# First unit's last pair with gates of its own, second unit's decays moved behind the first unit's masks, later weight merges on GpSimd

## The chip, the cores and the metric

The kernel runs on one core of one Trainium2 chip. The metric is the device time of one execution in microseconds (us); the time before is the median of three runs, 569.17 us (569.11 to 569.18). The profile is one execution under the hardware profiler, whose span is 567.4 us at a granted TensorE clock of 0.996. Engines: PE is TensorE, DVE is VectorE, ACT is ScalarE, POOL is GpSimd, SP is SyncE, which here only issues transfers.

## The reference, cut to what matters

The first half is a gated linear recurrence per batch entry and head, the second half a two-layer network with an ELU between the layers.

```python
f = 1.0 / (1.0 + np.exp(-f_logit))
for t in range(S):
    state = f[:, :, t, :, None] * state + np.einsum('bhd,bhe->bhde', k[:, :, t], v[:, :, t])
    y[:, :, t] = np.einsum('bhd,bhde->bhe', q[:, :, t], state)
h = x @ w_in
g = np.where(h > 0.0, h, alpha * (np.exp(np.minimum(h, 0.0)) - 1.0))
return (g @ w_out).astype(np.float32)
```

Sizes: 4 batch entries, 8 heads, 768 tokens, head size 48; x has 3072 rows of 384, the inner width is 2048. q, k, v and f_logit arrive as fp32, the weights as float64, and the kernel turns the weights into fp32 on the chip.

## The kernel before, in words

**Units.** The tokens are cut into 12 units of 256 (three per batch entry). For each unit q, k and f lie as 128 partitions x 4 head pairs x 256 tokens. 48 of every 64 partitions are real data, 16 are a gap. For f, the fourth pair (index `NKT` = 3) is not loaded into its own place before: its 96 rows go into the gaps beside the other three pairs (`load`, L437), so that the gates (exp and add) and the running products treat three pairs of 128 full partitions, and `move` (L629 to L634), an SBUF-to-SBUF transfer in two parts, then brings the result to the fourth pair's place.

**One unit's recurrence.** `gates` forms 1 + exp(-f_logit) on ACT (L608, L610). `grow` (L622) is a running product over the 256 tokens on DVE, `fall` (L627) its reciprocal on DVE. `scale` (L617) multiplies k by the product and q by its reciprocal on GpSimd. `transposed` (L665, L669) turns the scaled k on PE and copies it out on ACT, `advance` (L724) forms the state updates on PE, `step` (L682, L684, L687) sums them on DVE (the first one on ACT), `scores` (L701) is q times k on PE, `mask` (L709) applies the causal triangle on DVE. `outputs` and `carried` (L739, L759) form the unit's rows of x on PE, and ACT copies them out (L766, L768). For the very first unit `first_outputs` (L804 to L816) does the last two. `watch` (L646) only keeps a flag on the running products being in range.

**Weights.** Each of the 16 weight items (a 384 x 256 block of w_in, or a 256 x 384 block of w_out) is float64 when it lands in `area`, a ring of `AHEAD` = 7 places. `split` (L559, L563: two tensor_scalar operations on DVE) and `lower` (L569, ACT) prepare it, and `merge` (L577) adds the two 32-bit parts into the fp32 weight and then issues the fetch of the item seven further on. In order of need the items are: 0 wi0, 1 wi1, 2 wi2, 3 wo0, 4 wi3, 5 wo1, 6 wi4, 7 wo2, 8 wi5, 9 wo3, and so on. Before, all merges are on DVE: the integer add compiles to a custom DVE operation over 16-bit halves.

**Order.** Before the main loop the operations are written out by hand (L1037 to L1117); each engine runs its part in that order, and the SP queue issues transfers in that order. The main loop counts steps T. At even T = 2P it runs `up(P)` (x times a w_in block, L923 for the first two units), at odd T `down(P - 2)` (L955). A dictionary `plan` holds what else is done at which step: `attention(1, (), A1)` plans unit 1's advance, steps, scores with mask, outputs and carried at the steps named in A1, and `merge(n)` is planned two steps ahead of the item's first use, split and lower two steps before that. `warm` (L1032) are multiplications without a use that only keep TensorE busy. From unit 2 on, `up7` and `down` work with seven products instead of eight; that part isn't touched.

**DMA bookkeeping.** All transfers, of SP and of ACT, share eight completion semaphores in turn, so a transfer's issue waits until the transfer that had the same semaphore before it has landed. On the SP queue everything behind such an issue waits too.

Of the kernel before, what the change touches and what calls it, by code (L numbers as in the profile page):

```python
# [9 lines left out]
I32 = mybir.dt.int32  # L10
# [346 lines left out]
def fast(ctx: ExitStack, tc: tile.TileContext, q, k, v, f_logit, w_in, w_out, out, flag, outer):  # L357
# [36 lines left out]
    LAG = 2  # L394
    AHEAD = 7
    WA = 1
    W0 = 3
    HOLD = 2
    A1 = (2, 4, 4, 5, 7, 9)
    D2 = (14, 16, 18, 20)  # L400
    A2 = (22, 24, 24, 26, 27, 28)
    D3 = (-7, -5, -3, -1)
# [25 lines left out]
    def load(u, names="fkqv"):  # L428
        b, s0 = u // UPB, (u % UPB) * U
        for n in names.replace("v", ""):  # L430
            to = qkf[u % NB][n][MAIN]
            frm = src[n][b, :, :, s0 : s0 + U].rearrange("(p r) d s -> (r d) p s", r=2)
            if n == "f":
                to, frm = to[:, 0:NKT, 0], frm[:, 0:NKT]
            nc.sync.dma_start(out=to, in_=frm)
            for r in range(2 if n == "f" else 0):
# [14 lines left out]
    def blank(i, *engines, zeros=None):  # L451
        for j, e in enumerate(engines):
            w = HP // len(engines)
            for n in "kq":
                e.memset(qkf[i][n][:, j * w : (j + 1) * w], 0.0)
        (zeros or engines[-1]).memset(qkf[i]["f"][:, NKT], 1.0)

    start = ctx.enter_context(ExitStack())
    start.enter_context(tc.manual_schedule())
# [105 lines left out]
    def lower(n):  # L565

        if wide and n < NFT:
            raw = raws[n]
            nc.scalar.activation(raw.bitcast(U16)[:, 2::4], raw.bitcast(U32)[:, 0::2], AF.Copy, scale=2.0**-29)  # L569

    def merge(n):
        if wide and n < NFT:
            hi = raws.pop(n).bitcast(I32)[:, 1::2]
            j, out_ = parts[n]
            to = wo[:, 2 * j : 2 * j + 2] if out_ else wi[j][:]
            bits, hi = (x.rearrange("p (k f) -> p k f", k=to.shape[1]) for x in (held.pop(n)[:], hi))
            nc.vector.tensor_tensor(out=to.bitcast(I32), in0=bits, in1=hi, op=ALU.add)  # L577
        fetch(n + AHEAD)


# [22 lines left out]
    def gates(u, pieces=(NKT,), bias=1):  # L603

        p = 0
        for n in pieces:
            a = qkf[u % NB]["f"][:, p : p + n, 0]
            nc.scalar.activation(a, a, AF.Exp, scale=-1.0)  # L608
            if bias:
                nc.scalar.activation(a, a, AF.Copy, bias=1.0)  # L610
            p += n

    def scale(u, *todo):

        t = qkf[u % NB]
        for n, p, e in todo:
            e.tensor_tensor(out=t[n][:, p], in0=t[n][:, p], in1=t["f"][:, p, "kq".index(n)], op=ALU.mult)  # L617
# [27 lines left out]
    def watch(u):  # L645
        nc.vector.scalar_tensor_tensor(  # L646
            out=fine[:], in0=qkf[u % NB]["f"][:, 0:NKT, 0, U - 1 :], scalar=LIMIT, in1=fine[:],
            op0=ALU.is_le, op1=ALU.mult,
        )

# [39 lines left out]
    def scores(u, banks=("a0", "a1"), pairs=range(HP), pc=None):  # L690

        t = qkf[u % NB]
        if pc is None:
            ats[u] = sb.tile([128, 2, NW, HP, C], FP32, tag="at", name=f"at{u}", bufs=1)
            pc = [ps.tile([128, NW, HP, C], FP32, tag=banks[r], name=f"psS{u}_{r}") for r in range(2)]
        for p in pairs:
            for w in range(NW):
                for b in range(2):
                    cols = slice(w * W + b * C, w * W + b * C + C)
                    for r in range(2):  # L700
                        nc.tensor.matmul(  # L701
                            pc[r][FULL[b], w, p], lhsT=t["k"][FULL[r], p, cols], rhs=t["q"][FULL[r], p, cols],
                            start=True, stop=True,
                        )
        return pc
# [8 lines left out]
    def advance(u, pairs=range(HP)):  # L714

        if u not in pus:
            pus[u] = [ps.tile([128, NW, HP, D], FP32, tag=n, name=f"psU{u}_{n}") for n in ("a0", "a1")]
        pu = pus[u]
        for p in pairs:
            for w in range(NW):  # L720
                for r in range(2):
                    h = 2 * p + r
                    for b in range(2):
                        nc.tensor.matmul(  # L724
                            pu[b][FULL[r], w, p], lhsT=kns[u, p // 2][FULL[b], p % 2, w, FULL[r]],
                            rhs=vs[u % NB][FULL[b], w, PAD + h * D : PAD + (h + 1) * D],
                            start=(w == 0 and p == 0), stop=(w == NW - 1 and p == HP - 1), skip_group_check=True,
                        )
# [91 lines left out]
    def at_step(step, *todo):  # L820
        plan.setdefault(step, []).extend(todo)
# [206 lines left out]
    def warm(n, bank="m0"):  # L1028

        pw = ps.tile([128, 4, 128], FP32, tag=bank, name="psW")  # L1030
        for _ in range(n):
            nc.tensor.matmul(  # L1032
                pw[:], lhsT=ident[:], rhs=ident[:].unsqueeze(1).broadcast_to([128, 4, 128]), start=True, stop=True
            )


    gates(0, (1, 2))  # L1037
    fetch(0)
    load(1, "kqv")
    for n in range(1, HOLD):  # L1040
        fetch(n)
    warm(W0, "m3")
    for p in range(NKT):
        grow(0, p)
        scale(0, ("k", p, nc.gpsimd))
        if p < 2:
            transposed(0, 0, "m0", (p,))
    move(0, 0, nc.scalar)
    transposed(0, 1, "m1", (0,))
    fall(0, 0)  # L1050
    scale(0, ("q", 0, nc.gpsimd))
    warm(WA, "m3")
# [5 lines left out]
        vs[0][:, :, PAD : PAD + NKT * 2 * D].rearrange("t w (p r d) -> t w p r d", r=2, d=D)[:, :, :, 0],  # L1058
    )
    fall(0, 1)  # L1060
    scale(0, ("k", NKT, nc.gpsimd), ("q", 1, nc.gpsimd))
    fall(0, 2)
    move(0, 1, nc.scalar)
    warm(4)
    transposed(0, 1, "m1", (1,))
    advance(0, (2,))
    scores(0, None, (1,), pc)
    scale(0, ("q", 2, nc.gpsimd))
    advance(0, (3,))
    scores(0, None, (2,), pc)  # L1070
    nc.gpsimd.tensor_copy(
        padded_v[:, :, :, PAD : 2 * PAD].rearrange("t w (r j) k -> t w r j k", r=2),
        vs[0][:, :, PAD + NKT * 2 * D : PAD + DM].rearrange("t w (r k j) -> t w r j k", r=2, j=NKT),
    )
    a = qkf[1]["f"][:, 0:NKT, 0]
    nc.vector.tensor_scalar_add(a, a, 1.0)
    for p in range(NKT):
        grow(1, p)
    move(1, 0, nc.sync)
    scale(0, ("q", NKT, nc.gpsimd))  # L1080
    warm(2)
    scores(0, None, (NKT,), pc)
    warm(1)
    fall(1, 0)
    for c in range(NC - 1):
        step(0, c)
    mask(0, pc)
    step(0, NC - 1)
    split(0)
    for c in range(NC - 1):  # L1090
        nc.gpsimd.tensor_copy(
            padded_s[:, c, :, PAD : 2 * PAD],
# [4 lines left out]
        nc.gpsimd.memset(area[:, HOLD:].bitcast(I32)[:, :, 0:1], 0)  # L1097
# [12 lines left out]
    transposed(1, 1, "a1")  # L1110
    lower(1)
    watch(0)
    scale(1, ("q", 1, nc.gpsimd))
    fall(1, 2)
    scale(1, ("q", 2, nc.gpsimd))
    move(1, 1, nc.scalar)
    watch(1)  # L1117
    at_step(1, lambda: scale(1, ("q", NKT, nc.gpsimd)))
    attention(1, (), A1)
    for n in range(1, NFT):  # L1120
        t = max(needs[n][0] - 2, 0)
        at_step(t, lambda n=n: merge(n))
        if n > 1:
            later.setdefault(max(t - 2, 0), []).append(n)
    at_step(4, lambda: load(2))
# [89 lines left out]
```

## Time and profile before

| | us |
|---|---|
| time, median of three | 569.17 |
| span in the profile | 567.4 |
| PE busy | 550.2 (97%) |
| DVE busy | 395.2 (70%) |
| POOL busy | 266.3 (47%) |
| ACT busy | 229.3 (40%) |

The averages hide two stages. Up to some 45 us the recurrence of units 0 and 1 and the conversion of the first weights run, and PE waits now and then; from there on PE is without a gap up to the last microseconds. The page shows this in its 40 slices of 14.2 us: the first three digits of PE are 6, 8 and 7, all but the last of the others are 9. So the times of day in the first 60 us, in the timeline of each engine, are what has to be read: start, length, engine, line, tile, and in brackets how long the engine stood still before and what released it. A line of the DMA queue (SPq, ACTq) is the issue of a transfer, not the transfer.

### The profile page before, as it was taken

Reading aid. Unit: us, or ns where it says so; the run is one execution under the profiler, and the core shown is the slowest. Engines: PE = TensorE matmul, PEld = TensorE weight load, DVE = VectorE, ACT = ScalarE, POOL = GpSimd, SP = SyncE. Lnnn points to the kernel's source line nnn. Section 1 sums busy time; section 2 is a strip of 40 time slices with the busy share of each in tenths; the row PEclk is TensorE's granted clock in tenths of the full one; section 3 lists DMA queues with packets and bytes.
Section 4 is the critical chain, followed back from the end, with each engine's and each line's share of the span. In section 5 each row is a group of like instructions: output and inputs, shape, how many; then the busy total and the mean of one; then the engine's idle time right before and its main releaser. Section 6 shows DMA issues by size and latency. Waiting matters only on the chain.

```text
span 567.4 us, 15202 instructions
## 1 busy us (share of the span) xinstructions
PE 550.2 (97%) x6226; PEld 501.8 (88%) x6226; DVE 395.2 (70%) x765; ACT 229.3 (40%) x417; POOL 266.3 (47%) x530
## 2 busy tenths in 40 slices
PE   6879999999999999999999999999999999999996
PEld 3457777778999999999999999999999999999995
DVE  8798485835976795885785885786786876745543
ACT  3297737334343443434333343343333343333331
POOL 6510027642374474465366357257257348325332
PEclk9998999999999999999999999999999999999999
DMA  8989780060025125215216216216206203201001
GB/s 207 259 215 297 174 223 14 2 161 29 2 50 140 58 60 143 73 45 152 79 36 155 85 37 154 84 38 154 84 20 172 84 9 72 85 2 36 29 2 35
DMA packets 37902, 53.27 MB, mean 94 GB/s; under 512 B 3680, under 2 KB 27648, under 8 KB 37824
## 3 DMA queue, kind: packets, MB, share of 16 engines
q1 hardware_dynamic: 37024, 51.62, 34.6%
q8 instruction: 51, 0.84, 0.6%
q10 hardware_dynamic: 800, 0.59, 0.5%
q14 instruction: 27, 0.22, 0.1%
HBM read 44.04 MB, written 4.72 MB: 86 GB/s over the span
## 4 chain that ended last, share of the span: by engine, by line
PE 92%; DVE 3%; DMA 2%; issue 1%; ACT 1%; POOL 1%; SPq 0%; DVEq 0%; ACTq 0%; POOLq 0%
PE psH L878 35%; PE psM L977 33%; PE psM L955 8%; PE psH L923 6%; PE psS L701 2%; PE psY L739 2%; PE psY L759 2%; PE psU_a L724 2%; PE psT L665 2%; DMA f<-f 1%; DVE f L627 1%; DMA f<-in_f_logit_dram 1%; ACT area L569 1%; DVE bits L559 0%; PE psY L804 0%
## 5 line engine op out<-in xcount | busy, mean ns | idle before, releaser
L878 PE MATMUL psH<-xt,wi 128*128 128x128 f32 (+1 forms) x960 | 177.1, 293 | 0.0
L942 POOL TENSOR_TENSOR sums<-gg 128x128 f32<-128x128 f32 x160 | 69.5, 455 | 210.8 <-DVE gg L932 202.5
L878 PEld LDWEIGHTS psH<-xt,wi 128*128 128x128 f32 x960 | 135.9, 192 | 0.8
L910 ACT ACTIVATE gg<-hh 128x512 f32<-128x512 f32 x80 | 50.5, 631 | 205.9 <-DVE hh L900 140.5
L878 PE MATMUL psH<-xt,area 128*128 128x128 f32 x640 | 110.5, 275 | 0.0
L878 PEld LDWEIGHTS psH<-xt,area 128*128 128x128 f32 x640 | 96.9, 192 | 4.1
L887 DVE TENSOR_TENSOR hh<-psH,u 128x256 f32<-128x256 f32 x80 | 33.8, 423 | 88.7 <-ACT u L885 88.7
L977 PE MATMUL psM<-area,sums 128*128 128x192 f32 x480 | 91.2, 326 | 0.0
L977 PEld LDWEIGHTS psM<-area,sums 128*128 128x128 f32 x480 | 80.1, 190 | 0.2 <-POOL sums L942 0.2
L977 PE MATMUL psM<-wo,gg 128*128 128x192 f32 x320 | 68.1, 335 | 0.0
L617 POOL TENSOR_TENSOR k<-k,f 128x256 f32<-128x256 f32 x48 | 39.4, 822 | 57.1 <-DMA area<-in_moe_w_in_dram 35.0
L627 DVE RECIPROCAL f<-f 128x256 f32<-128x256 f32 x36 | 62.8, 1747 | 1.3
L911 ACT ACTIVATE gg<-gg 128x512 f32<-128x512 f32 x96 | 60.6, 631 | 3.0
L932 DVE SCALAR_TENSOR_TENSOR gg<-gg,hh 128x512 f32<-128x512 f32 x80 | 55.7, 696 | 1.8 <-ACT gg L911 1.8
L977 PEld LDWEIGHTS psM<-wo,gg 128*128 128x128 f32 x320 | 50.2, 190 | 1.9
L900 DVE TENSOR_TENSOR hh<-psH,u43h 128x256 f32<-128x256 f32 (+1 forms) x160 | 49.8, 353 | 2.7
L923 PE MATMUL psH<-xt,wi 128*128 128x256 f32 x192 | 44.5, 381 | 1.4 <-DVE wi L577 1.2
L942 POOL TENSOR_TENSOR sums<-gg,sums 128x128 f32<-128x128 f32 x80 | 42.8, 535 | 6.3
L955 PE MATMUL psM<-wo,gg 128*128 128x384 f32 x128 | 45.4, 498 | 0.0
L885 ACT COPY u<-psH 128x128 f32<-128x128 f32 x80 | 21.0, 263 | 59.3 <-PE psH L878 59.3
L923 PEld LDWEIGHTS psH<-xt,wi 128*128 128x128 f32 x192 | 35.9, 190 | 8.6 <-issue 1.6
L900 DVE TENSOR_TENSOR u43h<-psH,hh 128x256 f32<-128x256 f32 x80 | 33.9, 423 | 13.4 <-PE psH L878 13.0
(97 smaller groups left out, 721.9 us busy)
## 6 DMA issues: line engine op xcount, KB each, us to landing
area<-in_moe_w_out_dram SPq DMA_DIRECT2D x8, 768.0 KB, 8.9
again<-in_moe_w_in_dram SPq DMA_DIRECT2D x16, 384.0 KB, 4.1
again<-in_moe_w_out_dram SPq DMA_DIRECT2D x16, 384.0 KB, 3.5
k<-in_k_dram SPq DMA_DIRECT2D x12, 384.0 KB, 4.8
q<-in_q_dram SPq DMA_DIRECT2D x12, 384.0 KB, 5.5
v<-in_v_dram SPq DMA_DIRECT2D x12, 384.0 KB, 5.9
area<-in_moe_w_in_dram SPq DMA_DIRECT2D x8, 576.0 KB, 7.2
out_dram<-o SPq DMA_DIRECT2D x38, 96.0 KB, 1.7
```

The source lines that it names most:

```text
L617: e.tensor_tensor(out=t[n][:, p], in0=t[n][:, p], in1=t["f"][:, p, "kq".index(n)], op=ALU.mult)
L627: nc.vector.reciprocal(f[:, p, 1], f[:, p, 0])
L878: nc.tensor.matmul(to, lhsT=lhs, rhs=rhs, start=(n == 0), stop=True, skip_group_check=True)
L887: add = lambda to, x, y: nc.vector.tensor_tensor(out=to, in0=x, in1=y, op=ALU.add)
L900: add = lambda to, x, y: nc.vector.tensor_tensor(out=to, in0=x, in1=y, op=ALU.add)
L910: nc.scalar.activation(g[:], h, AF.Relu, scale=-1.0)
L911: nc.scalar.activation(g[:], g[:], AF.Exp, scale=-1.0)
L923: nc.tensor.matmul(ph[:, i], lhsT=wi[j][:, kt, i * 128 : (i + 1) * 128], rhs=xts[m][:, kt, :], start=(kt == 0), stop=(kt == NKT - 1),)
L932: nc.vector.scalar_tensor_tensor(out=g[:], in0=g[:], scalar=-1.0, in1=phs.pop(P), op0=ALU.add, op1=ALU.max)
L942: nc.gpsimd.tensor_tensor(out=s[:, i], in0=x, in1=y, op=op)
L955: nc.tensor.matmul(pm[t][:], lhsT=g[:, i, t * 128 : (t + 1) * 128], rhs=wo[:, 2 * j + i, :], start=(j == 0 and i == 0), stop=(j == NP - 1 ...
L977: nc.tensor.matmul(pm[bank][:, half * DH : (half + 1) * DH], lhsT=x, rhs=y, start=first, stop=(j == NP - 1), skip_group_check=True,)
```

## The change

Three things are done, with the retuning that goes with them.

1. Unit 0's fourth pair is loaded into its own place in one transfer with the others, the gaps of f are filled with 50.0 first (on GpSimd, so that their gates become 1), and gates, running product, scaling and reciprocal of unit 0 treat four pairs. The two `move` calls of unit 0 are gone, and with them the waits for these transfers. The price is a fourth grow and a fourth fall on DVE, one more pair in gates, and a `watch_last`.
2. Unit 1's add, running products and reciprocals stood on DVE between unit 0's falls and unit 0's masks; they now stand behind the masks and the first merge. split(0) goes ahead of the masks, merge(1) ahead of the main loop, unit 1's transposes, third fall and second move into step 1 of the loop. Steps 5, 7 and 8 replace 4, 5 and 7 for unit 1's steps, scores and outputs, and its last q scaling goes to step 4 (`Q1`).
3. Merges from item 3 on (`M0`) are integer adds on GpSimd.

```diff
+    M0 = 3
+    Q1 = 4
-    A1 = (2, 4, 4, 5, 7, 9)
+    A1 = (2, 4, 5, 7, 8, 9)
...
-            if n == "f":
+            if n == "f" and u:
                 to, frm = to[:, 0:NKT, 0], frm[:, 0:NKT]
+            elif n == "f":
+                to = to[:, :, 0]
...
-        (zeros or engines[-1]).memset(qkf[i]["f"][:, NKT], 1.0)
+        if i:
+            (zeros or engines[-1]).memset(qkf[i]["f"][:, NKT], 1.0)
+        else:
+            engines[-1].memset(qkf[i]["f"][:, :, 0], 50.0)
...
-            nc.vector.tensor_tensor(out=to.bitcast(I32), in0=bits, in1=hi, op=ALU.add)
+            e = nc.gpsimd if n >= M0 else nc.vector
+            e.tensor_tensor(out=to.bitcast(I32), in0=bits, in1=hi, op=ALU.add)
...
-    gates(0, (1, 2))
+    gates(0, (1, 1, 2))
...
-    for p in range(NKT):
+    for p in range(HP):
         grow(0, p)
         scale(0, ("k", p, nc.gpsimd))
-        if p < 2:
-            transposed(0, 0, "m0", (p,))
-    move(0, 0, nc.scalar)
-    transposed(0, 1, "m1", (0,))
+        transposed(0, p // 2, f"m{p // 2}", (p % 2,))
...
-    scale(0, ("k", NKT, nc.gpsimd), ("q", 1, nc.gpsimd))
+    scale(0, ("q", 1, nc.gpsimd))
     fall(0, 2)
-    move(0, 1, nc.scalar)
-    warm(4)
-    transposed(0, 1, "m1", (1,))
+    fall(0, 3)
...
+    scale(0, ("q", NKT, nc.gpsimd))
+    warm(1)
+    scores(0, None, (NKT,), pc)
+    warm(1)
+    split(0)
+    for c in range(NC - 1):
+        step(0, c)
+    lower(0)
+    mask(0, pc)
+    merge(0)
+    step(0, NC - 1)
     a = qkf[1]["f"][:, 0:NKT, 0]
     nc.vector.tensor_scalar_add(a, a, 1.0)
     for p in range(NKT):
         grow(1, p)
     move(1, 0, nc.sync)
-    scale(0, ("q", NKT, nc.gpsimd))
-    warm(2)
-    scores(0, None, (NKT,), pc)
-    warm(1)
-    fall(1, 0)
-    for c in range(NC - 1):
-        step(0, c)
-    mask(0, pc)
-    step(0, NC - 1)
-    split(0)
+    split(1)
...
+    first_outputs(0)
+    first_outputs(1)
+    warm(1)
+    lower(1)
+    fall(1, 0)
+    scale(1, ("k", 0, nc.gpsimd), ("k", 1, nc.gpsimd), ("k", 2, nc.gpsimd), ("q", 0, nc.gpsimd))
     fall(1, 1)
-    first_outputs(0)
-    lower(0)
-    merge(0)
-    first_outputs(1)
-    scale(1, ("k", 0, nc.gpsimd), ("q", 0, nc.gpsimd), ("k", 1, nc.gpsimd), ("k", 2, nc.gpsimd))
+    merge(1)
     scale(1, ("k", NKT, nc.gpsimd))
-    split(1)
-    transposed(1, 0, "a0")
-    warm(1)
-    transposed(1, 1, "a1")
-    lower(1)
     watch(0)
-    scale(1, ("q", 1, nc.gpsimd))
-    fall(1, 2)
-    scale(1, ("q", 2, nc.gpsimd))
-    move(1, 1, nc.scalar)
-    watch(1)
-    at_step(1, lambda: scale(1, ("q", NKT, nc.gpsimd)))
+    watch_last(0)
+    at_step(1, lambda: transposed(1, 0, "a0"), lambda: transposed(1, 1, "a1"))
+    at_step(1, lambda: scale(1, ("q", 1, nc.gpsimd)))
+    at_step(1, lambda: fall(1, 2))
+    at_step(1, lambda: scale(1, ("q", 2, nc.gpsimd)))
+    at_step(1, lambda: move(1, 1, nc.scalar))
+    at_step(1, lambda: watch(1))
+    at_step(Q1, lambda: scale(1, ("q", NKT, nc.gpsimd)))
```

In the changed kernel the fetch of items 2 to 6 and unit 1's first move keep their place in the text, but merge(0), and so the fetch of item 7, now stands ahead of them: on the SP queue the order becomes item 7, the two parts of unit 1's first move, item 2, 3, 4, 5, 6, item 8.

More of the change, by code (lines that the diff above doesn't have):

```diff
@@ L432, in load @@
             frm = src[n][b, :, :, s0 : s0 + U].rearrange("(p r) d s -> (r d) p s", r=2)
-            if n == "f":
+            if n == "f" and u:
                 to, frm = to[:, 0:NKT, 0], frm[:, 0:NKT]
+            elif n == "f":
+                to = to[:, :, 0]
             nc.sync.dma_start(out=to, in_=frm)
-            for r in range(2 if n == "f" else 0):
+            for r in range(2 if n == "f" and u else 0):
                 nc.sync.dma_start(
@@ L647, in watch, with watch_last @@
             out=fine[:], in0=qkf[u % NB]["f"][:, 0:NKT, 0, U - 1 :], scalar=LIMIT, in1=fine[:],
+            op0=ALU.is_le, op1=ALU.mult,
+        )
+    def watch_last(u):
+        nc.vector.scalar_tensor_tensor(
+            out=fine[:, 0:1], in0=qkf[u % NB]["f"][:, NKT:, 0, U - 1 :], scalar=LIMIT, in1=fine[:, 0:1],
             op0=ALU.is_le, op1=ALU.mult,
@@ L1074, in fast @@
     )
+    scale(0, ("q", NKT, nc.gpsimd))
+    warm(1)
+    scores(0, None, (NKT,), pc)
+    warm(1)
+    split(0)
[5 more added lines that the diff above has]
+    step(0, NC - 1)
     a = qkf[1]["f"][:, 0:NKT, 0]
@@ L1099, in fast @@
         fetch(n)
-    fall(1, 1)
-    first_outputs(0)
-    lower(0)
-    merge(0)
-    first_outputs(1)
-    scale(1, ("k", 0, nc.gpsimd), ("q", 0, nc.gpsimd), ("k", 1, nc.gpsimd), ("k", 2, nc.gpsimd))
-    scale(1, ("k", NKT, nc.gpsimd))
-    split(1)
-    transposed(1, 0, "a0")
-    warm(1)
-    transposed(1, 1, "a1")
-    lower(1)
-    watch(0)
-    scale(1, ("q", 1, nc.gpsimd))
-    fall(1, 2)
-    scale(1, ("q", 2, nc.gpsimd))
-    move(1, 1, nc.scalar)
-    watch(1)
-    at_step(1, lambda: scale(1, ("q", NKT, nc.gpsimd)))
+    first_outputs(0)
+    first_outputs(1)
+    warm(1)
+    lower(1)
+    fall(1, 0)
+    scale(1, ("k", 0, nc.gpsimd), ("k", 1, nc.gpsimd), ("k", 2, nc.gpsimd), ("q", 0, nc.gpsimd))
+    fall(1, 1)
+    merge(1)
+    scale(1, ("k", NKT, nc.gpsimd))
+    watch(0)
+    watch_last(0)
[6 more added lines that the diff above has]
+    at_step(Q1, lambda: scale(1, ("q", NKT, nc.gpsimd)))
     attention(1, (), A1)
@@ L1121, in fast @@
         t = max(needs[n][0] - 2, 0)
-        at_step(t, lambda n=n: merge(n))
+        if n > 1:
+            at_step(t, lambda n=n: merge(n))
         if n > 1:
```

## Prediction

> **What bounds the kernel now.** I read first the page's slices (PE full from the fourth slice on), then the timeline of each engine up to 65 us. PE:
>
> ```profile
> 37.35 2.83 PE L923 MATMUL psH<-xt,wi 128*128 128x256 f32 x12 [0.19 <-PE psU_a L724]
> 42.78 0.29 PE L701 MATMUL psS<-q,k 64*64 64x64 f32 x2 [2.60 <-issue]
> 43.29 1.72 PE L701 MATMUL psS<-q,k 64*64 64x64 f32 x62 [0.21 <-DVE state L682]
> 44.94 3.88 PE L955 MATMUL psM<-wo,gg 128*128 128x384 f32 x8
> 48.66 2.75 PE L923 MATMUL psH<-xt,wi 128*128 128x256 f32 x12
> ...
> 57.80 1.16 PE L759 MATMUL psY<-q,state 64*64 64x64 f32 x64
> ```
>
> The last gap of PE ends at 43.29 with unit 1's scores; behind it only PE work sets the end. From unit 1's `carried` (L759, 57.80) on, both kernels have the same PE work in the same order. So the gain is 57.80 minus the time at which the changed kernel starts it. What held the scores is DVE, one queue without air:
>
> ```profile
> 21.25 1.29 DVE L709 TENSOR_TENSOR at<-psS,twice 128x512 f32<-128x512 f32 x2 [2.42 <-POOL area L1097]
> ...
> 36.25 0.96 DVE L577 CUSTOM_DVE_ANT_0 wi<-area,bits 128x1536 uint16<-128x1536 uint16 x1 [0.41 <-ACT area L569]
> 37.24 0.97 DVE L559 TENSOR_SCALAR bits<-area 128x768 int32<-128x768 int32 x1
> ```
>
> The first line is unit 0's masks. The POOL operation named as their releaser only ended last; what they needed is PE's scores of the last pair, which end at 21.13 (timeline of PE), and those needed POOL's q scaling, which waited for unit 0's second `move`. The other two lines: merge(2) waits for ACT's lower, and a split beside a POOL operation takes 0.97. POOL:
>
> ```profile
> 19.89 0.72 POOL L617 TENSOR_TENSOR q<-q,f 128x256 f32<-128x256 f32 x1 [1.88 <-DMA f<-f]
> ...
> 36.46 1.33 POOL L617 TENSOR_TENSOR q<-q,f 128x256 f32<-128x256 f32 x1 [4.17 <-DMA f<-f]
> ```
>
> The first line is that q scaling; behind the second (unit 1's last one, also held by a `move`) POOL stands idle until 72.77, so there is room for merges. The queue of transfers, each line an issue:
>
> ```profile
> 21.25 0.32 SPq L542 DMA_DIRECT2D area<-in_moe_w_in_dram  x1
> ...
> 36.15 0.32 SPq L542 DMA_DIRECT2D area<-in_moe_w_in_dram  x1
> 36.51 1.20 SPq L545 DMA_DIRECT2D area<-in_moe_w_in_dram  x2
> ```
>
> Item 2 goes out at 21.25. Item 6 (36.15) goes out while the DMA engines are idle. By the DMA view, asked issue by issue, its three parts land 5.2, 5.5 and 5.3 us after their issues, the last at 42.4, which is 6.25 after the first issue. Items 7, 8, 9 and 10, queued behind it, land at about +10, +13.4, +15 and +18 from 36.15.
>
> **What the skill says.** The Trainium skill, GPSIMD Engine Reference, section 3.1 (Elementwise): a two-input elementwise add of 2048 fp32 takes 4497 ns on GpSimd; per element that agrees with this trace (128x128 0.455, 128x256 0.722: 2.09 ns an element). The same page, section 4.1 (Engine selection), calls a 32-bit integer add native there; no row here shows one. Its section 8 (Key points) says that GpSimd shares SBUF interfaces with VectorE operations of two inputs or in a 2-port mode; the trace agrees: L617 above took 1.33 instead of 0.72 beside L559, which took 0.97 instead of 0.56. The Trainium skill, TensorE: Matmul & The Clock Gate, Part 1 (The HAM clock gate): an idle window of some 3.4 us halves the clock. Here 2.6 us idle did: the windows of 1 us show 0.50 granted from 44 to 47 us, and L955 took 3.88 where it takes 2.74.
>
> **The change, step by step.**
>
> *Unit 0's load, +1.8.* f now waits for a POOL memset of 1024 columns: POOL's 512-column one takes 0.52, two 0.98, so it ends at 2.70 and f goes out at 2.76 instead of 0.80. 288 KB took 3.1; with 96 KB more at the page's 260 GB/s 3.5: landed 6.3 (before 4.6). Gates (0.42+0.42 a pair, 0.61+0.63 for two): pairs 2 and 3 at 9.15; the third and fourth grow end at 10.6 instead of 8.4.
>
> *DVE up to the masks, -2.* Four falls at 1.66: 17.3. split(0) 1.3, two steps 0.75: 19.35. Before, unit 1's add 0.62, three grows 1.86 and one fall 1.73 stood here, and then everything waited until the second move had landed at 19.8. POOL's last q scaling ends at 18.1, its scores at 18.7, so the masks run 19.3 to 20.55 (before 21.25 to 22.54). The moves of unit 0 cost nothing now.
>
> *DVE behind the masks.* merge(0) 0.95 (lower(0), 1.95 on ACT, hides behind steps and masks) 21.5; last step 0.95; add 0.62; grows 1.9: 24.95; split(1) 1.1; two falls 3.3; merge(1) 0.95: 30.3. watch_last is 0.1 in a wait below: nothing. PE: first_outputs takes 5.0 from the masks' end as before, x is out at about 27, up(0) 27.0 to 29.7, transposes to 30.8, up(1) 30.8 to 33.4 (before 33.25 to 36.0). Here the change is 2.6 ahead.
>
> *The wait that replaces the old ones: item 2.* On SP item 7 and unit 1's first move now stand ahead of item 2. The move waits for the grows (24.95), is issued in two parts of 0.63, so item 2 goes out at 26.3, not 21.25. Like item 6 before, it lands 6.25 later: 32.55. DVE, there at 30.4, waits: split(2) ends at 33.7. Behind it in the queue: fall(1,2) (35.4), and on ACT everything:
>
> lower(2) 33.7-35.6, two kn copies 36.65 (advance waits), the second move's issue 37.9, lower(3) 39.8, gate pair gg (0.6+0.63) 41.1, lower(4) 43.0, lower(5) 44.9, gg 46.2, lower(6) 48.1, lower(7) 50.2 (its split ends 48.3), gg 51.5, lower(8) and (9) at 1.9 each 55.3, the two `between` copies 0.47: 55.8. `carried` waits for these, so it starts at **55.85**. ACT is the bound from 33.7 on, by its own rows of the timeline. Items 3, 4, 5, 6 and 8, at the spacing of the burst from 36.15, land at 36.3, 39.7, 41.3, 44.3 and 47; each split takes 1.1 and so is ready (37.4, 40.8, 42.4, 45.4) just before ACT comes to its lower: close, and no wait of its own.
>
> *PE and POOL beside it.* advance at about 36.2, after 2.8 idle: a cold clock is likely, and hidden, since up(2) (merge(2) on DVE 38.9) ends by 42 even slowed and down(0) needs merge(3). POOL merge, bounds: 0.95 (DVE's row) to 3.3 (1.79 times the 1.84 of the disturbed row); 768 elements at 2.09 ns from 0.722 give 1.79, taken as 1.9. merge(3): 39.8 to 41.7. Then q's last scaling, ahead of merge(4) in POOL's queue, waits for the second move (second part out at 37.3, landing 5.2 later, as before): 42.5, 43.2. merge(4) 45.1, up(3) 45.15. From there PE alone needs up 2.65, scores 1.09, down 2.6, outputs 1.09, up 2.6: 55.2, so ACT, not PE, is last by 0.65. DVE saves 0.95 per merge, and, more, its splits and steps no longer stand behind merges that wait for ACT (before, the steps ended only at 43.15). The other edits (retuned warms, 50.0, A1) carry no further cost: PE waits at those places.
>
> Sum: 57.80 - 55.85 = 1.95; 569.17 - 1.95 = **567.2**. Behind carried: down(2), up(5), down(3) run to 64.7, and unit 1's rows of x (copies to 58.6, transfer issued by 58.7, 5.0 to land) are there at 63.7. POOL's later merges have steps of 2.6 us each for 1.9: hidden.
>
> **Rivals.**
> - *Item 2 is not waited for.* If f is quicker or SP issues sooner so that item 2 is there at 30.4, ACT's chain starts 2.1 sooner: carried at 53.7, gain 4.1, **565.1**. For it: 768 KB at 260 GB/s are 2.9 us, and only item 7 is in flight. Against it: item 6's 6.25 on idle engines.
> - *GpSimd becomes the bound.* With 3.3 a merge: merge(3) 43.1, scaling 43.8, merge(4) 47.1, carried at 47.1+10.05 = 57.15, gain 0.6, **568.5**. For it: all splits are of the 2-port kind. Against it: only part of the time is a split running.
> - *Slower.* In the burst from 21.25 item 2 landed at 29.7, 8.45 after its first issue. Like that it lands at 34.75, and ACT's chain puts carried at 58.05; with merges disturbed by another 0.7 on the way, 58.8: 1.0 later than before, 570.2; a cold clock behind the longer PE gap (it cost 1.1 in L955 and 0.6 in the scores before) adds up to 1.7: **571**. For it: the gap before advance would be 5 us. Against it: the slow landing came from parts issued 2.6 us apart.
>
> **How the numbers follow.** Forecast 0.54, item 2 early 0.18, GpSimd bound 0.15, slower 0.13. The forecast's own spread is about 1 us (f's landing, each DVE operation beside POOL), so a small part of it falls under 1.1 us: faster 0.68, same 0.19, slower 0.13. The range leaves out the far half of the early case and most of the slower one: 565.0 to 569.4.
>
> **What would show it.** Right: masks at about 19.3; SP issuing item 2 behind unit 1's move near 26; split(2) waiting for DMA to about 32.5; ACT without a gap from there to `between` near 55.5; carried near 55.9; GpSimd merges of 1.8 to 2.2. Wrong: split(2) not waiting for a transfer, merges over 3 us, up(3) waiting beyond 46, or PE gaps behind 57.

## The result and the profile after

The changed kernel takes **575.55 us** (574.94 to 575.99, 4 runs) where the kernel before, on the same chip, takes 569.14 (568.74 to 569.18): ratio 1.0113, 95% interval 1.0096 to 1.0131. That is 6.4 us slower; 567.2 was predicted. The profiled spans are 573.2 (after) and 567.4 (before).

The timeline of PE of the kernel after. Columns: start, us, engine, line, operation, operands, count, and in brackets the idle time before with what ended it. Here and below, only the rows that the text needs are shown.

```profile
34.57 2.83 PE L937 MATMUL psH<-xt,wi 128*128 128x256 f32 x12 [0.58 <-DVE wi L585]
40.07 0.31 PE L738 MATMUL psU_a<-v,kn 64*64 64x48 f32 x2 [2.67 <-ACT kn L683]
42.26 4.54 PE L937 MATMUL psH<-xt,wi 128*128 128x256 f32 x12 [0.57 <-DVE wi L585]
46.64 2.74 PE L969 MATMUL psM<-wo,gg 128*128 128x384 f32 x8
49.65 2.86 PE L937 MATMUL psH<-xt,wi 128*128 128x256 f32 x12 [0.27 <-POOL wi L585]
53.62 1.59 PE L715 MATMUL psS<-q,k 64*64 64x64 f32 x64 [1.11 <-issue]
59.21 0.32 PE L753 MATMUL psY<-at,v 64*64 64x64 f32 x2 [1.22 <-DVE at L723]
64.03 1.34 PE L773 MATMUL psY<-q,state 64*64 64x64 f32 x64 [0.28 <-ACT between L760]
```

`carried` (L773) starts at 64.03, not at 57.80 as before. That is 6.23 later, and it holds the whole loss: from there to the end of the span it is 509.2 us (before 509.6). So the prediction compared the right instant and gave it the wrong time: 55.85 was forecast. TensorE waits often ahead of it: the larger gaps are 2.67, 0.57, 0.27, 1.11 and 1.22, where the kernel before, from `up(2)` on, had one gap of 2.60 and one of 0.21 and then ran full.

The timeline of DVE, after: the masks of unit 0 (L723), the split of item 2, the second half of split(4), split(6), the second half of split(7), and split(9).

```profile
22.61 1.29 DVE L723 TENSOR_TENSOR at<-psS,twice 128x512 f32<-128x512 f32 x2 [1.87 <-PE psS L715]
36.44 0.56 DVE L566 TENSOR_SCALAR bits<-area 128x768 int32<-128x768 int32 x1 [1.23 <-DMA area<-in_moe_w_in_dram]
43.05 2.08 DVE L570 TENSOR_SCALAR area<-area 128x768 int32<-128x768 int32 x1
49.63 2.18 DVE L566 TENSOR_SCALAR bits<-area 128x768 int32<-128x768 int32 x1 [2.85 <-POOL wi L585]
54.81 2.08 DVE L570 TENSOR_SCALAR area<-area 128x768 int32<-128x768 int32 x1
60.83 0.56 DVE L566 TENSOR_SCALAR bits<-area 128x768 int32<-128x768 int32 x1 [1.07 <-POOL wo L585]
```

Three things stand here. The masks come 1.36 later than before, not 2 sooner, and wait for TensorE's scores. Split(2) waits for item 2's transfer, as forecast, but 3.9 later than forecast. And splits now wait for POOL, and halves of them take 2.1 or 2.2 instead of 0.56: neither was in the prediction.

The timeline of POOL, after: q's last scaling of unit 0, merge(3), q's last scaling of unit 1, merge(4), merge(5), merge(6).

```profile
17.90 0.91 POOL L625 TENSOR_TENSOR q<-q,f 128x256 f32<-128x256 f32 x1 [0.51 <-DVE f L635]
42.79 1.92 POOL L585 TENSOR_TENSOR wo<-bits,area 128x768 int32<-128x768 int32 x1 [2.47 <-ACT area L576]
47.06 0.73 POOL L625 TENSOR_TENSOR q<-q,f 128x256 f32<-128x256 f32 x1 [2.35 <-DMA f<-f]
47.74 1.85 POOL L585 TENSOR_TENSOR wi<-bits,area 128x768 int32<-128x768 int32 x1
49.55 1.84 POOL L585 TENSOR_TENSOR wo<-bits,area 128x768 int32<-128x768 int32 x1
54.44 2.04 POOL L585 TENSOR_TENSOR wi<-bits,area 128x768 int32<-128x768 int32 x1 [3.05 <-ACT area L576]
```

A merge on GpSimd takes 1.84 to 2.04; 1.9 was taken. Now lay the two timelines on each other. The split half at 43.05 starts beside the merge at 42.79 and ends at 45.13, 0.42 behind that merge's end (44.71). Split(6) ends at 51.81, 0.42 behind the merge that ends at 51.39. The half at 54.81 ends at 56.89, 0.41 behind 56.48. Such a half is not slowed by some factor: it ends only 0.4 after the merge beside it.

The SP queue, after: unit 1's first move, and the first part of item 2 behind it.

```profile
28.48 1.30 SPq L642 DMA_DIRECT2D f<-f  x2
29.87 0.53 SPq L549 DMA_DIRECT2D area<-in_moe_w_in_dram  x1
```

### The profile page after: what moved, and what is told of

The parts are those of the page before. It is cut to its first block, busy times and chain, and to the rows that moved or that the text cites. A ratio compares the mean times of both kernels' runs of the same rounds, so it can differ in the third digit from the quotient of the medians.

```text
span 573.2 us, 15184 instructions
## 1 busy us (share of the span) xinstructions
PE 552.4 (96%) x6220; PEld 502.8 (88%) x6220; DVE 394.0 (69%) x755; ACT 229.9 (40%) x419; POOL 292.0 (51%) x543
## 4 chain that ended last, share of the span: by engine, by line
PE 89%; DMA 3%; DVE 3%; POOL 2%; issue 1%; ACT 1%; SPq 0%; ACTq 0%; DVEq 0%; POOLq 0%
PE psH L892 34%; PE psM L991 33%; PE psM L969 6%; PE psH L937 5%; PE psS L715 2%; PE psU_a L738 2%; PE psY L773 2%; PE psY L753 2%; PE psT L679 2%; DMA f<-f 1%; PE psW L1046 1%; DMA area<-in_moe_w_in_dram 1%; POOL wi L585 1%; DMA f<-in_f_logit_dram 1%; DVE bits L566 1%
## 5 line engine op out<-in xcount | busy, mean ns | idle before, releaser
L635 DVE RECIPROCAL f<-f 128x256 f32<-128x256 f32 x37 | 64.2, 1745 | 1.0
L937 PE MATMUL psH<-xt,wi 128*128 128x256 f32 x192 | 46.5, 394 | 1.9 <-DVE wi L585 1.1
L969 PE MATMUL psM<-wo,gg 128*128 128x384 f32 x128 | 44.2, 488 | 0.0
```

The costliest lines, as they stand in the source:

```text
L937: nc.tensor.matmul(ph[:, i], lhsT=wi[j][:, kt, i * 128 : (i + 1) * 128], rhs=xts[m][:, kt, :], start=(kt == 0), stop=(kt == NKT - 1),)
L969: nc.tensor.matmul(pm[t][:], lhsT=g[:, i, t * 128 : (t + 1) * 128], rhs=wo[:, 2 * j + i, :], start=(j == 0 and i == 0), stop=(j == NP - 1 ...
```

## The experiments

All of them compute everything that the reference asks for. The kernel before was timed beside each set: 569.46, 568.88 and 569.77 us median. Ratios are against it. A second reading is the start of `carried` in the profile; a table at the end of the section lists it. It is one execution of each kernel, so it has a spread too. The changed kernel and three variants of it are the same up to merge(3), yet their profiles have the masks at 22.61, 22.83, 23.12 and 21.66; five variants with W0 = 5 (all but the one that also moves f's memset) have them between 20.08 and 20.43. A difference of one or two us in a single profile is therefore not shown by it alone.

**The head: TensorE's clock.** The windows of the kernel after show it (from:to, length, busy us of PE, PEld, DVE, ACT, POOL with counts, granted clock of TensorE, DMA share, GB/s):

```profile
11.00:12.00 1.00, 0.08 (x1) 0.08 (x2) 1.00 (x2) 0.37 (x1) 1.00 (x2) 0.79 1.09 315
12.00:14.00 2.00, 1.45 (x5) 1.02 (x6) 2.00 (x2) 0.52 (x2) 1.48 (x3) 0.50 1.06 260
14.00:16.00 2.00, 2.00 (x22) 0.55 (x24) 2.00 (x2) 0.97 (x2) 0.88 (x2) 0.50 1.12 198
16.00:18.00 2.00, 2.00 (x57) 1.75 (x50) 2.00 (x3) 0.00 (x0) 1.20 (x3) 0.50 1.14 268
```

The warming products of the start end at 8.75. From there TensorE has only the first transposes, since f comes later:

```profile
9.59 0.44 PE L679 MATMUL psT<-ident,k 128*128 128x128 f32 x2 [0.83 <-POOL k L625]
10.58 0.41 PE L679 MATMUL psT<-ident,k 128*128 128x128 f32 x2 [0.55 <-ACT kn L683]
11.92 0.69 PE L679 MATMUL psT<-ident,k 128*128 128x128 f32 x2 [0.93 <-POOL k L625]
```

It works 0.85 us between 8.75 and 11.6, where the clock halves (0.79 is the mean from 11 to 12). Up to 18.4 it then does unit 0's other transposes, advances, scores and warming products at half the clock. The last scores start at 22.03, 3.2 after POOL's scaling for them ended. The first experiment fills the start with two more warming products.

```diff
-    W0 = 3
+    W0 = 5
```

> Changed kernel with five instead of three warming multiplications at the start. Theory A (TensorE goes cold at 11.7 us because the first transposes come at 9.6 with gaps, and its slow advances, warmings and scores then put the masks at 22.6 instead of 19.3 to 20): clock full from 8 to 23 us, masks near 20, item 2 out some 2.5 us sooner, time 572.5 to 573.5. Theory B (masks are late from POOL's scalings and DVE's falls, a cold clock is beside it): masks above 22, 575 to 576.

Measured: 573.38 us, ratio 1.0078 (1.0047 to 1.011). The windows and the masks of this kernel:

```profile
12.00:14.00 2.00, 1.35 (x7) 0.74 (x8) 2.00 (x2) 0.91 (x3) 1.48 (x3) 1.00 1.08 253
16.00:18.00 2.00, 2.00 (x36) 0.85 (x34) 2.00 (x2) 0.32 (x1) 1.11 (x2) 1.00 1.12 237
```

```profile
20.43 1.29 DVE L723 TENSOR_TENSOR at<-psS,twice 128x512 f32<-128x512 f32 x2
34.60 0.56 DVE L566 TENSOR_SCALAR bits<-area 128x768 int32<-128x768 int32 x1 [1.21 <-DMA area<-in_moe_w_in_dram]
```

This is theory A. The clock stays full, the masks come 2.2 sooner (no wait ahead of them any more) and `carried` 1.75 sooner. The profiles named above agree: the masks come last in the three where half the clock lasts 6.8 us (22.61 to 23.12), sooner in the fourth, where it lasts 3.4 us (21.66), and soonest in the five with no half clock at the head. The half clock at the head is thus shown to cost about 1.7 at `carried`.

**The head: f's later load.** On top of that, f's own memset is put first on GpSimd, so that its transfer leaves sooner.

```diff
+        if not i:
+            engines[-1].memset(qkf[i]["f"][:, :, 0], 50.0)
         for j, e in enumerate(engines):
...
-        else:
-            engines[-1].memset(qkf[i]["f"][:, :, 0], 50.0)
```

> The kernel of a_w5 with the memset of unit 0's f put ahead of k's and q's on GpSimd, so that its transfer leaves about 0.9 sooner (1.8 instead of 2.7). Theory A (the later load of f is on the path to the masks, as forecast): grows, falls, masks and item 2 each about 0.9 sooner than in a_w5 (masks near 19.5, item 2 near 27.5), carried near 61.4; time 572.3 to 572.8. Rival B (VectorE is ahead of something else at the head, for instance the clock of TensorE): masks within 0.3 of 20.4 and a time of 573.1 to 573.6.

Measured: masks at 19.54, `carried` at 61.18, 1.1 sooner than with W0 = 5 alone; span 571.1 against 571.8. The time is 573.01 us, ratio 1.0064 (1.0046 to 1.0082): the ratios of the two kernels overlap, so the gain is not shown in the times. The masks are 0.5 or more ahead of those in all five other profiles with W0 = 5, so the place of f in GpSimd's queue of memsets is on the path to them. But with f 0.9 sooner than the forecast took it, the masks are still 0.24 later than the forecast 19.3.

**Item 2 ahead of the move.** On top of W0 = 5, items 2 and 3 are fetched ahead of merge(0), so SP issues them before item 7 and unit 1's first move.

```diff
     lower(0)
     mask(0, pc)
+    if wide:
+        nc.gpsimd.memset(area[:, HOLD:].bitcast(I32)[:, :, 0:1], 0)
+    fetch(HOLD)
+    fetch(HOLD + 1)
     merge(0)
...
-    for n in range(HOLD, AHEAD):
+    for n in range(HOLD + 2, AHEAD):
```

> The changed kernel with W0=5 and items 2 and 3 fetched ahead of merge(0), so that on SP they stand in front of item 7 and of unit 1's first move. Theory A (the order on SP makes split(2) wait): item 2 is issued at 21 to 23 instead of 28.4 and landed by 28; split(2) starts right behind the second fall of unit 1, near 33.4, 1.2 sooner than with W0=5 alone; carried near 61.0 (62.28 with W0=5 alone); time 571.5 to 572.5. Rival B (behind split(2) the chain of splits, merges on GpSimd and lowers sets the time, whatever it starts from, since later items or the second move come in late): split(2) starts sooner but carried stays within 0.4 of 62.28; time 573 to 574.

Measured: 573.11 us, ratio 1.0065 (1.0046 to 1.0083), span 572.3. Split(2) waits for nothing now and starts at 32.29, 2.3 sooner, yet `carried` is at 63.14, not sooner than with W0 = 5 alone (62.28). The timeline of this kernel shows what took the place of the wait:

```profile
32.29 0.56 DVE L566 TENSOR_SCALAR bits<-area 128x768 int32<-128x768 int32 x1
36.09 0.72 POOL L625 TENSOR_TENSOR k<-k,f 128x256 f32<-128x256 f32 x1 [5.62 <-DMA f<-f]
42.97 0.56 DVE L566 TENSOR_SCALAR bits<-area 128x768 int32<-128x768 int32 x1 [3.31 <-POOL wo L585]
```

The two parts of unit 1's first move, now issued behind two weight items, took 9.4 us to land instead of the 2.8 of the kernel with W0 = 5. GpSimd's scaling of k stands behind the move, TensorE's last transposes and ACT's copies of them behind the scaling, and lower(3) behind those on ACT. It starts at 39.08 (39.24 with W0 = 5 alone), so merge(3) and split(5) come hardly sooner (41.09 against 41.25, 42.97 against 43.46). Rival B was right here: an earlier start alone brings nothing. The same kernel with its merges on VectorE:

```diff
-    M0 = 3
+    M0 = 16
```

> The kernel of a_w5_i2 with every merge on VectorE again (M0=16). Leaves of the change only its first two parts, with the two faults of the start mended. Theory A (GpSimd merges cost some 2 us between split(2) and carried): carried 2 to 2.5 sooner than in a_w5_i2, near 58.7; time 569.5 to 570.5 unless unit 1's x comes in late again, which would give back up to 1.8. Rival B (merges on either engine are hidden behind the lowers): carried within 0.5 of that of a_w5_i2 and the same time.

Measured: 571.07 us, ratio 1.004 (1.0027 to 1.0052), `carried` at 57.12; up(1,0), the first product of unit 1, then waits 1.19 for unit 1's x. Its slowest run of 17 (572.82) is below the fastest of the four with merges on GpSimd (572.85), and the medians are 2.0 apart: theory A. The two profiles are 6.0 apart at `carried`, but that is not all the edit's. Unit 1's first move, the same in both kernels, landed sooner here:

```profile
34.20 0.73 POOL L625 TENSOR_TENSOR k<-k,f 128x256 f32<-128x256 f32 x1 [3.85 <-DMA f<-f]
```

That is 1.9 ahead of 36.09, and lower(3) starts 1.9 sooner (37.18), before the first merge that differs, so at most 4.1 is left for the edit. This profile is also 1.1 below the median of its kernel and the other one 0.9 above. So `carried` 0.7 ahead of the kernel before doesn't show a gain either: the first two parts of the change with their faults mended stay slower than the kernel before, by 0.27 to 0.52%. How much of that is the wait for x was not tried.

**The third part by itself**, in the kernel before.

```diff
-            nc.vector.tensor_tensor(out=to.bitcast(I32), in0=bits, in1=hi, op=ALU.add)
+            e = nc.gpsimd if n >= 3 else nc.vector
+            e.tensor_tensor(out=to.bitcast(I32), in0=bits, in1=hi, op=ALU.add)
```

> Kernel before with merges from item 3 on put on GpSimd and nothing else changed: the third part of the change alone. Theory A (GpSimd merges lose by themselves through waits of splits for merges and the shared port): slower than before by 1 to 4 us, 570 to 573, with splits waiting for GpSimd in the trace. Theory B (they save DVE 0.95 us each and DVE was the bound): faster than before by 1 to 3 us, 566 to 568.

Measured: 571.6 us, ratio 1.0029 (1.0015 to 1.0044), span 569.9, `carried` at 60.84 (before 57.80). From its timeline:

```profile
40.33 0.56 DVE L559 TENSOR_SCALAR bits<-area 128x768 int32<-128x768 int32 x1 [2.43 <-POOL wo L578]
40.46 2.12 POOL L578 TENSOR_TENSOR wi<-bits,area 128x768 int32<-128x768 int32 x1 [0.16 <-ACT area L569]
40.93 2.08 DVE L563 TENSOR_SCALAR area<-area 128x768 int32<-128x768 int32 x1
44.83 2.42 PE L702 MATMUL psS<-q,k 64*64 64x64 f32 x64 [5.14 <-issue]
```

So the part that was to help VectorE costs time even where nothing else changes: 3.0 at `carried` in the profile, 2.1 between the medians. A split waits for a merge; the next half of it runs beside the following merge and ends 0.43 after it (43.01 against 42.58); the steps come later, and TensorE's gap ahead of the scores grows from 2.60 to 5.14.

**All merges on VectorE in the changed kernel** (M0 = 16, as above).

> Changed kernel with all merges on DVE as before. Theory A (GpSimd merges cost more than they give: the chain over two engines and two buffers, and splits of 2.1 instead of 0.56 us beside a merge): DVE runs as in the kernel before from split(2) to carried, 24.8 us, from 36.4 on, so carried at 61.2 instead of 64.0 and 572.7. Theory B (GpSimd merges relieve DVE and it is the head that lost): 576 to 578.

Measured: `carried` at 61.82, 2.2 sooner, as theory A said. But the span is 573.2, as with merges on GpSimd, and the time 574.86 us, ratio 1.0092 (1.0065 to 1.0119): no gain is shown. From its PE timeline:

```profile
61.82 1.35 PE L773 MATMUL psY<-q,state 64*64 64x64 f32 x64
72.87 2.83 PE L937 MATMUL psH<-xt,wi 128*128 128x256 f32 x12 [1.76 <-DMA xt<-xt]
```

Unit 1's x is an SBUF-to-SBUF transfer of two parts; here they took 6.6 and 7.6 us beside the weight items and the load of unit 2's k, q and v (before: 5.0 median), so up(1,0) waits. To test that, the same kernel loads k, q and v later:

```diff
-    at_step(4, lambda: load(2))
+    at_step(4, lambda: load(2, "f"))
+    at_step(10, lambda: load(2, "kqv"))
```

> The changed kernel with all merges on VectorE (M0=16) and unit 2's k, q and v loaded from step 10 on. Theory A (merges on GpSimd cost 2.2 up to carried, and without them the gain was lost to unit 1's x alone, 1.76 of wait): carried at about 61.8, no wait at up(1,0), time 572.6 to 573.4. Rival B (something else gives the gain back): 574.3 to 575.3.

Measured: `carried` at 61.73, x lands in 6.0, the wait is gone and the span is 571.1, 2.1 shorter. The time is 573.51 us, ratio 1.0082 (1.0057 to 1.0107). The profile is theory A's; in the times the two ratios overlap. `carried` is where it was although the masks came 1.5 sooner in this profile than in the last one; 1.2 of that went into half the clock at up(2), which took 4.09 here and 2.86 there. Two profiles of the changed kernel with merges on GpSimd (64.03, and 64.04 below) and two without (61.82, 61.73) thus give the same 2.2.

**Which of GpSimd's couplings costs.** A split writes the buffer `bits`, a ring of two, which the merge two items earlier reads. With merges on GpSimd that is a wait of DVE for POOL. First, four buffers:

```diff
+    BB = 4
...
-tag="bits", name=f"bits{n}")
+tag="bits", name=f"bits{n}", bufs=BB)
```

> Changed kernel with four instead of two buffers for the bits that split writes and merge reads. Theory A (with merges on GpSimd, a split waits for the GpSimd merge two items earlier, because it writes the buffer that merge still reads): the waits of 2.8, 1.1 and 1.2 us of splits 6, 9 and 10 for GpSimd go, split(6) starts when item 6 is there, near 47.8 instead of 49.6, unit 1's steps behind it start some 2 us sooner, and the time falls by 1.5 to 3 us from 575.5, to 572.5 to 574. Theory B (the loss is all at the head, late masks and so late items; the later waits only follow): 575 to 576.

Measured: 574.91 us, ratio 1.0094 (1.0066 to 1.0122), `carried` at 64.04: nothing. The timeline:

```profile
48.03 1.84 POOL L586 TENSOR_TENSOR wi<-bits,area 128x768 int32<-128x768 int32 x1
48.23 2.06 DVE L567 TENSOR_SCALAR bits<-area 128x768 int32<-128x768 int32 x1 [1.23 <-DMA area<-in_moe_w_in_dram]
49.83 2.15 POOL L586 TENSOR_TENSOR wo<-bits,area 128x768 int32<-128x768 int32 x1
50.33 2.08 DVE L571 TENSOR_SCALAR area<-area 128x768 int32<-128x768 int32 x1
```

The wait for merge(4) is gone, split(6) starts 1.4 sooner, and both its halves now run beside a merge, each ending 0.42 or 0.43 behind it. The merge between them, started while the first half still ran, waits in its turn: it takes 2.15 instead of 1.84 and ends 1.69 after that half. The steps begin at 52.33 (after: 52.32). The wait was replaced by its like.

Second, with W0 = 5, q's last scaling behind merge(4) in GpSimd's queue instead of ahead of it:

```diff
-    Q1 = 4
+    Q1 = 5
```

> The changed kernel with W0=5 and Q1=5: unit 1's last q scaling, which waits for the second move, comes behind merge(4) in GpSimd's queue instead of ahead of it. Theory A (GpSimd's queue held merge(4), and through it up(3) and split(6)): merge(4) starts at about 43.4, right behind merge(3), up(3) at about 45.5 instead of 47.89, split(6) at about 45.5 instead of 47.87, carried at about 60.2 instead of 62.28; time 571.2 to 572.2. Rival B (behind it the scores of unit 1, which need that scaling, or the slow splits beside merges are last): up(3) sooner, carried at 61.5 or later; time 572.7 to 573.6.

Measured: 573.25 us, ratio 1.0071 (1.0046 to 1.0095), `carried` at 62.41 (62.28 without): rival B. Here split(4) fell beside merge(3) (`40.85 2.21` where it was 0.56), so lower(4) and merge(4) came no sooner (45.72 against 45.99). Third, both together:

> The kernel of a_w5_q5 with four buffers for the bits that split leaves for merge (two before). No split waits for a merge on GpSimd any more; splits still run beside merges and are slow there. Theory A (with q's scaling out of the way the wait for the buffer is what is left): carried another 0.8 to 1.5 sooner than in a_w5_q5, time 570.0 to 571.3. Rival B (a split beside a merge takes 2.1 instead of 0.56, so it ends no sooner, as in a_bits4): carried within 0.4 of a_w5_q5, same time.

Measured: 572.92 us, ratio 1.0066 (1.0045 to 1.0087), span 570.5, `carried` at 60.53: 1.9 sooner than with Q1 = 5 alone and 1.75 sooner than with W0 = 5 alone, of which 0.39 goes to a wait for x. The direction is theory A's, the time is not (570.0 to 571.3 was expected), and the medians of the two kernels with Q1 = 5 are only 0.3 apart. In this profile split(2), which neither edit reaches, is already 0.5 sooner than with W0 = 5 alone (34.11 against 34.60). So 1.3 to 1.6 at `carried` is what the two edits can claim together, from one profile; neither alone gave any of it.

**A version that beats both kernels, the one before by 0.3%.** The kernel before has a gap of 2.60 ahead of unit 1's scores, behind which the clock is half. It is filled with warming products:

```diff
+    at_step(5, lambda: warm(3, "m3"))
     attention(1, (), A1)
```

> The kernel before with three warming matmuls put ahead of unit 1's scores, into the gap of 2.6 us that TensorE has there. Theory A (the half clock from 43.3 to 47 costs 1.1 in the down product and 0.6 in the scores, all on the path): L955 takes 2.75 instead of 3.88, carried near 56.3 instead of 57.8; time 567.4 to 567.9. Rival B (behind the gap other work is last, the splits and lowers of items 7 to 9, or the warming matmuls end late and hold the scores): carried at 57.3 to 57.8, time 569.0 to 569.6.

Measured: 568.62 us, ratio 0.9987 (0.9974 to 1.0), span 566.9. The PE timeline:

```profile
44.17 2.85 PE L955 MATMUL psM<-wo,gg 128*128 128x384 f32 x8
55.99 1.16 PE L759 MATMUL psY<-q,state 64*64 64x64 f32 x64
66.47 2.83 PE L923 MATMUL psH<-xt,wi 128*128 128x256 f32 x12 [1.37 <-DMA xt<-xt]
```

L955 takes 2.85 instead of 3.88 and `carried` starts 1.81 sooner, but x took 7.2 to land and 1.37 of it is given back. It is the same loss as above, so the same edit of the load was added:

> The kernel of b_warm with unit 2's k, q and v loaded from step 10 on instead of step 4 (f stays at step 4). Theory A (in b_warm the gain of 1.8 at carried was lost to unit 1's x, whose transfer took 7.2 beside the load of k, q and v): the transfer of x takes 4.5 to 5.5, up(1,0) does not wait, the gain stays: time 567.0 to 567.6 where the kernel before has 568.9 to 569.2. Rival B (the weight items alone keep the DMA engines full, or unit 2's k comes in late and costs as much): x takes over 6.5 or a new wait stands near 75 to 85; time 568.4 to 569.4.

```profile
56.03 1.16 PE L759 MATMUL psY<-q,state 64*64 64x64 f32 x64
65.00 2.83 PE L923 MATMUL psH<-xt,wi 128*128 128x256 f32 x12
```

x lands in 5.7 and up(1,0) does not wait. Measured: **567.52 us** (567.06 to 569.09, 9 runs) where the kernel before has 569.77: ratio 0.9968, interval 0.9955 to 0.9981. The intervals of this kernel and of the one without the late load overlap, so the times show the gain of the pair, not the share of each edit. It takes over nothing of the change.

All profiles in one table (us). The last column takes `carried` and the wait for x at up(1,0) off the span.

| kernel | carried | span | wait for x | span - carried - wait |
|---|---|---|---|---|
| before | 57.80 | 567.4 | - | 509.6 |
| after | 64.03 | 573.2 | - | 509.2 |
| W0 = 5 | 62.28 | 571.8 | - | 509.5 |
| W0 = 5, f's memset first | 61.18 | 571.1 | - | 509.9 |
| W0 = 5, items 2, 3 first | 63.14 | 572.3 | - | 509.2 |
| the same, merges on VectorE | 57.12 | 568.1 | 1.19 | 509.8 |
| before, merges on GpSimd | 60.84 | 569.9 | - | 509.1 |
| after, merges on VectorE | 61.82 | 573.2 | 1.76 | 509.6 |
| the same, late load | 61.73 | 571.1 | - | 509.4 |
| after, four bits buffers | 64.04 | 573.6 | - | 509.6 |
| W0 = 5, Q1 = 5 | 62.41 | 571.6 | - | 509.2 |
| the same, four bits buffers | 60.53 | 570.5 | 0.39 | 509.6 |
| before, warming products | 55.99 | 566.9 | 1.37 | 509.5 |
| the same, late load | 56.03 | 565.8 | - | 509.8 |

The last column stays between 509.1 and 509.9 in fourteen profiles: what sets the span is `carried` and that one wait.

## Why the prediction was wrong

**What bounds the kernel now.** Right: the gain is the shift of `carried`. Not complete: it was said that behind it x comes in time. In the changed kernel it did, but in four of the kernels with an earlier `carried` x was late, by 0.39 to 1.76.

**"Unit 0's load, +1.8".** Nearly right: f landed at 6.6 (6.3 forecast), the last grow ended at 11.3 (10.6).

**"DVE up to the masks, -2".** This step failed first: masks at 22.61, not 19.3, so 3.3 late, which alone is more than the whole forecast gain of 1.95. 0.7 of it comes from the step before. Most of the rest is TensorE: the sum took the scores to follow POOL's scaling by 0.6, a figure of a full clock, and they started 3.2 behind it. It did not ask what the later f leaves TensorE to do between 8.75 and 11.92. With W0 = 5 the masks come 2.2 sooner, so about 2.2 of the 3.3 is shown to be the clock; the remaining 0.4 was not pursued. The prediction did weigh a cold clock, but only behind the later gap at 36 us, and called that one hidden. There it was right: up(2) took 4.54 instead of 2.86, and up(3) still waited 0.27 for its weights.

**"The wait that replaces the old ones: item 2".** Right in kind and nearly in size: SP issued item 2 7.3 behind the masks (7.0 forecast), and split(2) started 6.6 behind that (6.25). Its lateness of 3.9 is the 3.3 of the masks plus these two rests. The early rival gave an earlier item 2 its full worth at `carried`. Where item 2 was put in front of the move, that was not so: the move came in late instead.

**"PE and POOL beside it".** This step failed next, and cost as much again: it put the price of GpSimd merges for VectorE at nothing. The duration of a merge was right (1.84 to 2.04, taken as 1.9). Three things around it were not:

- The second move's last part went out at 40.05 (37.3 forecast), so 2.75 of the 3.9 arrived here, and landed 7.0 later, not 5.2. q's scaling, merge(4) and up(3) came 4.5 late: the 3.9 and 0.6 more.
- The step counted what VectorE saves and not what it waits for: split(n) writes the buffer that merge(n-2) reads. No such wait showed while both stood on one engine in order; it is not in the diff, only in the ring's length of two.
- The price of sharing was put on GpSimd ("bounds: 0.95 to 3.3" for a merge) and not on VectorE, though the trace of before had a split of 0.97 for 0.56 beside a POOL operation, quoted in the prediction itself. That split started at 37.24 and ended at 38.21, 0.42 behind L617 (36.46 + 1.33), the same 0.42 as in the trace of after. The Trainium skill, GPSIMD Engine Reference, section 8 (Key points), says that GpSimd contends for its SBUF interfaces with VectorE's operations of a 2-port mode or of two SBUF inputs, and this case shows how: the operation that starts second waits for the end of the first. The prediction misread its own line here. L617 took 1.33 because it started at 36.46 beside VectorE's merge(2) (36.25 to 37.21) and ended 0.58 behind it; the split of 0.97 then waited for L617. A split half that starts during a merge pays the merge's whole remaining time; a merge that starts during a half pays the half's, up to 0.4 here.

From up(3) to `carried` the forecast had 10.70, the trace has 14.38: 3.7 late. 3.9 + 0.6 + 3.7 is the whole miss of 8.2 at `carried`. Of the 3.7, 2.9 is TensorE standing still: 1.11 ahead of the scores, which come with VectorE's steps behind split(6); 1.22 and 0.27 ahead of the outputs, which wait for masks behind split(7) and split(8); 0.28 for ACT. Merging on VectorE gave 2.2 back in the changed kernel, 3.0 in the kernel before, and at most 4.1 in the one with items 2 and 3 first; taking two of GpSimd's couplings away (q's scaling ahead of merge(4), the ring of two) gave 1.3 to 1.6 in one profile. How the rest of the 3.7 divides between slow splits and the later state steps was not separated: no kernel here has GpSimd merges without slow splits.

**The claim "ACT is the bound"** fell with that step: ACT's lowers wait 1.36, 2.51 and 2.57 for splits between 45 and 57 us. The forecast summed ACT's own durations and took splits as ready.

```profile
45.16 3.68 ACT L576 ACTIVATE area<-area 128x768 uint16<-128x768 uint32 x2 [1.36 <-DVE area L570]
52.44 1.92 ACT L576 ACTIVATE area<-area 128x768 uint16<-128x768 uint32 x1 [2.51 <-DVE area L570]
56.93 1.93 ACT L576 ACTIVATE area<-area 128x768 uint16<-128x768 uint32 x1 [2.57 <-DVE area L570]
```

**The rivals.** "Slower" (571) was right in direction, in good part by luck: its first term, item 2 landing after 8.45, did not come (6.6), and its cold clock stood at the later gap, where it was hidden, not at the head. Its disturbed merges are the one term that fits, at 0.7 far too small. "GpSimd becomes the bound" (568.5) named the engine, but through a merge of 3.3 that does not exist: that figure scales a merge by the misread 1.33. Merges are not too slow, they shut out the splits. The forecast's own sign of being wrong, "up(3) waiting beyond 46", is what the trace shows (it starts at 49.65).

## What to carry to other kernels

Moving one operation to an idle engine turns the order within an engine into waits between two: look for the buffers that producer and consumer share, and count the ring, before counting the time saved. Where it runs beside operations that the trace shows waiting for it, as the splits here, charge its whole remaining duration to them. And a later input must be followed to TensorE as well: in these traces two or three microseconds with little to do were mostly followed by half the clock. A gain further on lasts only if the next transfer, here unit 1's x, comes in time too. A single profile has a spread of its own: before reading a difference at the end, compare the two at a point ahead of the edit.

## What the hardware showed that was not expected

- **The later of the two is locked out, not slowed.** An int32 tensor_scalar of 128x768, SBUF to SBUF, takes 0.56 alone. Started during a GpSimd tensor_tensor it ended 0.38 to 0.48 behind it in all 117 cases of the fourteen profiles, and took up to 2.2. It works the other way too: a GpSimd merge (1.84 alone) that started during such an operation ended 1.69 to 1.76 behind it, in all 32 cases. The masks (a tensor_tensor with an operand in PSUM) ran beside a merge in the same trace in 1.28, as ever.
- **Thin work halves the clock like idling.** In the kernel after, 0.85 us of work spread over 2.85 us, with no gap over 0.93, was followed by a clock of 0.50 from 11.6 to 18.4. The prediction had looked for gaps of some 2.6 us only. Two more warming products at the start kept it at 1.00. No fixed length shows: the gap of 2.3 ahead of unit 1's advance was followed by half the clock in the profile with the late load and merges on VectorE (up(2) took 4.09), and not in the one without the late load (2.86).
- **Small transfers depend on what is under way.** The two parts of unit 1's first move (48 KB each) landed 2.2 to 9.4 us after their issue (medians), by kernel; unit 1's x 2.3 to 7.2. With two weight items issued ahead, that move took 9.4 and 7.6 in two profiles, instead of 2.2 to 2.8 in the other changed kernels.
